# Pre-LN attention block with gated MLP: the end of each chunk through TensorE transposes, new ranks for residual sums and LN2, and the first K maximum from PSUM

## The chip, the cores and the metric

The kernel runs on one core of one Trainium2 chip. The metric is the device time of one execution in microseconds. Three runs of the kernel before gave 883.87, 884.46 and 886.01 us, median 884.46.

## The reference

One sequence of 2048 tokens, model width 640, 32 heads of 20, MLP width 1728, all inputs bf16. Random inputs are scaled by 0.05 (and the MLP weights by one over the root of their input width).

```python
def _A_ref(x, wqkv, wo):                       # attention
    qkv = (x @ wqkv).reshape(B, S, 3, H, Dh).transpose(2, 0, 3, 1, 4)
    q, k, v = qkv[0], qkv[1], qkv[2]
    scores = jnp.einsum("bhqd,bhkd->bhqk", q, k) * (Dh ** -0.5)
    p = softmax(scores)
    o = jnp.einsum("bhqk,bhkd->bhqd", p, v)
    return o.transpose(0, 2, 1, 3).reshape(B, S, D) @ wo

def _B_ref(x, w_gate, w_up, w_down):           # gated MLP
    return (gelu(x @ w_gate) * (x @ w_up)) @ w_down     # tanh form of gelu

h  = x + _A_ref(layernorm(x), wqkv, wo)
h2 = h + _B_ref(layernorm(h), w_gate, w_up, w_down)
```

The scores are 32 x 2048 x 2048 numbers, and each needs an exponential.

## The kernel before

**A planner writes the order.** The kernel first lists its operations (`op`) with engine, planned duration, priority, what each reads and writes, and which PSUM banks it takes and gives back. `Sched.schedule` then plays them through in planned time: whenever an engine is free it takes the ready operation with the lowest priority number (ties by the order of listing). `emit` writes each engine's program in exactly that order, with semaphore waits. So each engine's order is fixed before the kernel runs, and priorities act only through it. SP issues all DMAs, and one that has to wait holds back those behind it. `QK_LEAD`, `PE_AGE`, `SD_AGE`, `SD_ROW`, `DRAIN` are constants of this planner: how long before ScalarE runs dry TensorE takes no low-ranked work, how long an operation of another tiling mode may wait, and so on.

**Prologue.** x is loaded in four parts, normalized (LN1), transposed by TensorE into `xnT`. K and Q of the first group of four heads are projected first (`proj_k(0)`, `proj_q(0, 0)`). Scores are not shifted by their own row maximum: `q_bound0` computes a bound from the largest absolute value of each K row and |q|, and writes it into a spare row of Q, so the score matmul subtracts it. In `proj_k` this maximum takes, for each of four chunks of 512 columns, a copy from PSUM by ScalarE (L708), a bit mask on VectorE for the absolute value, a maximum with the first chunk's, and then one more fold and a reduction into `kd`; `sel0` is scaled by it and `q_bound0` multiplies.

**Middle.** The queries go in eight chunks of 512, 256 (five), 128 and 128 tokens. A chunk is worked in slots: chunk 0 has eight, a chunk of 256 four, one of 128 two; 32 slots (0 to 31) in all, each of 64 tiles of 128 keys x 512 scores. Slots 0 to 7 are chunk 0, slots 28 and 29 chunk 6, slots 30 and 31 chunk 7. `unit` takes tiles from the list by turns into three banks and two banks of PSUM (scores at L976, 32-row tiling) and lets ScalarE take the exponential of the whole unit into `pts` or `pts2`, a ring of `PR` + `PR2` tiles. `D_SLOT` gives the number of groups of four tiles in each slot whose exponential VectorE makes instead (`d_exp`): a conversion to int16 from PSUM (L889), then four shifted patterns whose bf16 readings sum to the exponential, each a separate operand of probability times V (`pv_op`); `SUMS` has some pairs of patterns added on VectorE first. All slots accumulate into one bank, bank 6; row 20 of each head holds the sum of the probabilities.

**End of a slot** (`epilogue`, `spread`): VectorE copies the bank to `osb`. For chunks 0 to 6 the sums go to DRAM and back in another layout, POOL takes reciprocals (ten instructions), these go to DRAM and come back broadcast over partitions (`bsum`), VectorE multiplies (`on16`, rank `P_ON`), and four DMAs write the rows to DRAM (`attn`). Chunk 7 (`tail`) does it with four fp32 TensorE transposes (L1063), a reciprocal (L1069) and products (L1072) into `o_nat`.

**After a chunk** (`post`): one DMA fetches the transposed attention output into `oT`, then follow the out projection, residual sum (L1124), LN2 statistics, a reciprocal root on POOL, `xn_t`, a DMA transpose into `hnT`, gate matmuls, gelu, up matmuls, product, down matmuls, the last sum into `ob` (L1228) and the output DMA. For chunks of 256 and more these matmuls run as four column tiles of 32 (`col4`, L676), for the last two chunks plain (L1158, L1223, L681). The work has ranks `P_LN` = 2.5 and `P_BG` = 3 and banks 5 and 7, so it fills the gaps that scores (0) and probability times V (1) leave; VectorE's patterns rank `P_EPI` = 2. `prefetch(c)` loads x of chunk c into its place of `h_sb`, which has room for four tiles of 128 tokens; chunks of 256 take its halves by turns. The MLP width is 13.5 tiles of 128: tile 13 overlaps tile 12 by half, and the doubled rows of w_down are zero.

Where TensorE would have nothing to do the planner writes matmuls whose results nobody uses (`warm`, operands from `kt_all`, and `pad`, zero weights added into bank 6).

The lines that the steps touch: `proj_qk` L701, `proj_k` L715, `q_bound0` L790, `proj_v` L802, `spread` L1023, `epilogue` L1044, `prefetch` L1078, `post` L1101.

## Time and profile before

| | us |
|---|---|
| median of three runs | 884.46 |
| profiled execution | 884.74 |
| its span | 883.0 |
| PE busy | 830.0 (94%) |
| ACT busy | 832.0 (94%) |
| DVE busy | 753.4 (85%) |
| POOL busy | 134.2 (15%) |
| mean share of the DMA engines in use | 20% |

PE is TensorE, ACT ScalarE, DVE VectorE, POOL GpSimd, SP SyncE, which issues the DMAs. A row of a group gives the line, the engine, the operation, what it writes from what, shapes and count; then busy time and the mean duration of one in ns; then the engine's idle time ahead of them and what ended it. The line can be that of a helper (L395 stands for all operations that were recorded through `I`). A row in order of time gives start, duration, engine, line, operation, and in brackets the idle time ahead of it. A row of stages gives, after the stretch and its length, the busy time and the number of instructions of PE, PE's weight loads, DVE, ACT and POOL, the clock granted to TensorE (1.00 is full speed), the DMA share and GB/s. Matmul durations of the profile include their pipeline, so matmuls that follow each other overlap.

### The profile page before, as it was taken

How to read it: one execution, taken by the hardware profiler on the slowest of the kernel's cores; microseconds unless marked ns; L12 is line 12 of the kernel's file. 1: busy time of each engine (PE TensorE's matmuls, PEld its weight loads, DVE VectorE, ACT ScalarE, POOL GpSimd, SP SyncE). 2: the span in 40 equal slices, each digit the busy share in tenths (PEclk: the TensorE clock that was granted, in tenths of full speed). 3: DMA queues.
4: the chain of work that ended last, by engine and by line, in shares of the span. 5: the costliest groups of instructions: out<-in, count | busy, mean ns of one | idle time of the engine just before them, and what ended most of it. 6: DMA issues, size and time to landing. Idle time of an engine off the chain costs nothing.

```text
span 883.0 us, 36651 instructions
## 1 busy us (share of the span) xinstructions
PE 830.0 (94%) x16658; PEld 405.4 (46%) x16658; DVE 753.4 (85%) x1356; ACT 832.0 (94%) x798; POOL 134.2 (15%) x431
## 2 busy tenths in 40 slices
PE   3999999999989899999999999999999999999998
PEld 1532222222234333344545555545554556666687
DVE  8839999999879889788899878999899997976864
ACT  6799999999999999999999999999999999999931
POOL 5001111110201201111031211113101321120200
PEclk9999999999999999999999999999999999999999
DMA  7211130332264410001121101101020101103000
GB/s 268 75 44 58 31 79 19 107 90 68 76 175 126 106 30 19 19 8 42 42 64 35 33 17 50 34 8 35 27 57 20 30 19 42 45 16 65 6 17 24
DMA packets 57298, 46.95 MB, mean 53 GB/s; under 512 B 25524, under 2 KB 50704, under 8 KB 57144
## 3 DMA queue, kind: packets, MB, share of 16 engines
q1 hardware_dynamic: 57144, 44.62, 19.2%
q8 instruction: 130, 2.13, 1.0%
q14 instruction: 24, 0.20, 0.1%
HBM read 30.68 MB, written 11.04 MB: 47 GB/s over the span
## 4 chain that ended last, share of the span: by engine, by line
ACT 56%; PE 28%; DVE 12%; POOL 1%; issue 1%; DMA 1%
ACT pts L395 44%; ACT rege L395 12%; PE ps L676 9%; PE ps L976 7%; PE ps L395 5%; PE ps L681 4%; DVE qt_all L395 3%; DVE rege L889 2%; PE ps L1158 2%; DVE rege L395 2%; DVE qt_all L889 1%; DVE stats L395 1%; PE ps L1223 1%; DMA rege<-xn_t 1%; ACT qt_all L395 1%
## 5 line engine op out<-in xcount | busy, mean ns | idle before, releaser
L395 ACT ACTIVATE pts<-ps 128x1024 bf16<-128x1024 f32 (+1 forms) x585 | 639.3, 1244 | 8.0 <-PE ps L976 6.1
L976 PE MATMUL ps<-qt_all,kt_all 32*128 32x256 bf16 (+2 forms) x4096 | 301.2, 272 | 24.3 <-ACT pts L395 17.5
L976 PEld LDWEIGHTS ps<-qt_all,kt_all 32*128 32x128 bf16 x4096 | 101.8, 92 | 227.1 <-ACT pts L395 150.5
L395 ACT ACTIVATE rege<-ps 128x1536 bf16<-128x1536 f32 (+1 forms) x129 | 178.6, 1401 | 1.7 <-PE ps L395 1.5
L889 DVE TENSOR_SCALAR rege<-ps 128x512 int16<-128x512 f32 x220 | 148.7, 682 | 27.9 <-PE ps L976 27.2
L676 PE MATMUL ps<-rege,regw 128*32 128x256 bf16 (+1 forms) x3360 | 152.4, 292 | 5.7 <-ACT rege L395 1.8
L395 PE MATMUL ps<-pts,v_all 128*21 128x256 bf16 (+2 forms) x2711 | 132.1, 273 | 0.3 <-ACT pts L395 0.2
L395 PE MATMUL ps<-rege,v_all 128*21 128x256 bf16 (+2 forms) x1877 | 130.1, 287 | 2.3 <-issue 1.5
L889 DVE TENSOR_SCALAR qt_all<-ps 128x512 int16<-128x512 f32 x136 | 92.2, 683 | 19.7 <-PE ps L976 18.8
L676 PEld LDWEIGHTS ps<-rege,regw 128*32 128x32 bf16 x3360 | 77.9, 96 | 44.5 <-issue 24.9
L395 DVE TENSOR_SCALAR rege<-rege 128x2048 int16<-128x2048 int16 x139 | 93.3, 684 | 2.5 <-PE ps L395 1.9
L681 PE MATMUL ps<-regw 128*128 128x512 bf16 (+1 forms) x360 | 90.2, 356 | 2.5 <-ACT regw L628 2.0
L395 POOL TENSOR_SCALAR rn<-rc 128x16 int32<-128x16 int32 x30 | 8.6, 288 | 526.2 <-DMA rc<-sums 525.8
L395 PEld LDWEIGHTS ps<-pts,v_all 128*21 128x21 bf16 x2711 | 62.4, 91 | 30.1 <-issue 23.3
L676 PE MATMUL ps<-regw,rege 128*32 128x320 bf16 x1568 | 74.7, 301 | 0.6 <-DVE rege L889 0.5
L395 DVE TENSOR_SCALAR qt_all<-qt_all 128x2048 int16<-128x2048 int16 (+2 forms) x118 | 68.8, 594 | 0.6
L395 PEld LDWEIGHTS ps<-rege,v_all 128*21 128x21 bf16 x1877 | 50.1, 91 | 36.4 <-issue 20.9
L395 PE MATMUL ps<-qt_all,v_all 128*21 128x256 bf16 (+1 forms) x1360 | 58.8, 262 | 0.5 <-DVE qt_all L395 0.3
L395 DVE TENSOR_SCALAR qt_all<-rege 128x2048 int16<-128x2048 int16 x83 | 56.2, 689 | 1.6 <-PE ps L395 1.0
L681 PEld LDWEIGHTS ps<-regw 128*128 128x128 bf16 x360 | 29.3, 99 | 51.1 <-issue 26.6
L1211 DVE TENSOR_TENSOR rege<-rege,ps 128x512 bf16<-128x512 bf16 (+1 forms) x53 | 35.8, 677 | 12.1 <-PE ps L676 11.2
L676 PEld LDWEIGHTS ps<-regw,rege 128*32 128x32 bf16 x1568 | 36.6, 96 | 19.0 <-issue 9.3
(113 smaller groups left out, 724.2 us busy)
## 6 DMA issues: line engine op xcount, KB each, us to landing
bsum<-rsums SPq DMA_DIRECT2D x120, 64.0 KB, 2.1
rege<-in_A_x_dram SPq DMA_DIRECT2D x5, 640.0 KB, 5.6
q_rows<-regw SPq DMA_DIRECT2D x20, 128.0 KB, 1.8
out_dram<-rege SPq DMA_DIRECT2D x16, 160.0 KB, 2.6
attn<-on SPq DMA_DIRECT2D x120, 20.0 KB
regw<-in_B_w_gate_dram SPq DMA_DIRECT2D x5, 432.0 KB, 3.6
regw<-in_B_w_up_dram SPq DMA_DIRECT2D x5, 432.0 KB, 3.3
kt_all<-k_rows SPq DMA_DIRECT2D x12, 160.0 KB
```

Source lines behind the costliest of these rows:

```text
L395: return lambda eng: getattr(eng, method)(*args, **kwargs)
L676: return [lambda eng, j=j: eng.matmul(out()[32 * j:32 * j + 32], l[:, 32 * j:32 * j + 32], r, start=start, stop=stop, tile_position=(0, 32 ...
L681: fn = col4(lambda: bank(bk, n), l, r, k == 0, k == len(steps) - 1) if col else lambda eng, l=l, r=r, k=k: eng.matmul(bank(bk, n), l, r, s ...
L889: d_ops.append(op("dve", lambda eng: eng.tensor_scalar(v[:, 512 * h:512 * h + 512], bank(b), EXP_MUL, -32000.0, ALU.mult, ALU.max), c_dve( ...
L976: return lambda eng: eng.matmul(out()[:, kk * nq:(kk + 1) * nq], kt_all[32 * j:32 * j + 32, g, kt * 128:(kt + 1) * 128], qt_all[32 * j:32 ...
L1158: lambda eng, a=a, f=f, fi=fi: eng.matmul(bank(bk)[:, fi * nq:(fi + 1) * nq], w[:, a, F0[f]:F0[f] + 128], hnT[:, a, 128 * tb:128 * tb + nq ...
L1211: hdone.append(op("dve", lambda eng, bu=bu, fv=fv, w=w: eng.tensor_tensor(fv, fv, bank(bu, w), ALU.mult), c_dve(w), p, reads=[ku] + hkeys( ...
L1223: f == NF - 1) if nq >= COL else lambda eng, f=f, o=o, hf=hf, bk=bk: eng.matmul(
```

## The change

- **Last slot of a chunk.** For chunks 1 to 6 the last slot, for chunk 0 slots 6 and 7, no longer go through DRAM. They take chunk 7's way (four fp32 transposes, reciprocal, products), into `wda` or `sq`, and small matmuls against the identity then transpose them into `oT`, with a VectorE copy. The other slots' rows still come by DMA, now two a chunk.
- **Ranks.** Out projection `P_OUT` 1.1, residual sums `P_ADD` 0.6, statistics and LN2 `P_ST` 0.7, the new transposes `P_NOW` 0.9 and their VectorE work `P_DV` 0.5, against 2.5 before. LN2 of chunks 0 and 3 is transposed by TensorE and copied by VectorE.
- **First K maximum.** VectorE reduces each chunk with absolute values to one column of `km`, the last one straight from PSUM before ScalarE copies it; one small reduction combines the four.
- **V.** Four first-half V tiles are copied by ScalarE (two before); VectorE's V copies and those of the second K tile wait for `sel0`. The second half of V moves from slots 0 to 2 to slots 1 and 2.
- **Last MLP tile.** For chunks of 256 and more tile 13 computes only its 64 columns, for both halves of the tokens at once, in half as many columns; `wda` holds the matching rows of w_down.
- **Output.** The last sum goes into `h_sb`, and the output DMA reads it there; `ob` is gone, and its space goes to `pts2`.
- **Numbers.** The ring has 13 + 6 tiles (12 + 4 before). Slot 30 has no VectorE tiles (two groups before). `SUMS`, `D_RING`, `D_SPAN` and the planner's constants get values by slot.

```diff
-PR, PR2 = 12, 4
-D_SLOT = (0,) + (3,) * 27 + (2, 3, 2, 1)
-SUMS = (0,) + (1,) * 6 + (0, 1, 1, 0) + (1,) * 5 + (2,) + (1,) * 10 + (0, 1, 1, 1, 0)
+PR, PR2 = 13, 6
+D_SLOT = (0,) + (3,) * 27 + (2, 3, 0, 1,)
+SUMS = (0,) + (1,) * 7 + (0, 1, 0,) + (1,) * 3 + (0, 1,) + (2,) * 3 + (1,) * 6 + (2, 1, 0, 1, 0, 1, 0,)
-VN = 6
-D_RING = (6,) * 26 + (4, 6, 12, 12, 0, 6)
-D_FIRST, D_SPAN = 0, 18
+VN = 3
+D_RING = (6,) * 8 + (9, 6, 6, 9,) + (6,) * 6 + (0, 6,) + (3,) * 7 + (6,) * 4 + (9,)
...
-V_ACT = (0, 1)
-XN_DVE = (9, 13, 15)
+V_ACT = (0, 1, 2, 3)
+XN_DVE = (12, 14, 15)
+HOLD = 1
+V_HOLD = 3
+XP_PE = (0, 3)
+P_NOW = 0.9
+P_K0 = 1.0
+P_DV = 0.5
+P_ADD = 0.6
+P_ST = 0.7
+P_OUT = 1.1
...
@@ proj_qk
-            if evac == "act":
+            if dkey[0] == "ku" and t == 0:
+                red = lambda src, r: op("dve", lambda eng: eng.tensor_reduce(km[:, c:c + 1], src(), AX.X, ALU.max, apply_absolute_value=True),
+                                        0.62, P_K0, reads=[r], writes=[("km", c)])
+                m = [red(lambda: bank(bk), key)] if c == 3 else []
+                e = op("act", lambda eng: eng.activation(dst, bank(bk), ACT.Copy), c_act(512), prio, reads=[key],
+                       writes=[dkey], rel=[bk], after=m)
+                if c < 3:
+                    w_readers.append(red(lambda: dst, dkey))
+            elif evac == "act":
...
@@ proj_k
+                op("dve", I("tensor_reduce", kd[:, 0:1], km[:], AX.X, ALU.max), 0.1, P_K0, reads=[("km", c) for c in range(4)],
+                   writes=[("kd", 0)])
...
@@ epilogue
-            if c < len(CHUNKS) - 1:
+            tail = c == len(CHUNKS) - 1
+            g_dir = [g for ss, (cc, gg) in enumerate(slots) if cc == c and (tail or gg[-1] == NG - 1 or c == 0 and gg[0] == NG - 2)
+                     for g in gg]
+            if gs[0] not in g_dir:
                 spread(s, c, gs, nq)
                 return
...
+            if tail or not last:
+                return
...
+            op("sp", I("dma_start", oT[:, 0:na, tok], src[0:128 * na, :].rearrange("(a p) s -> p a s", p=128)), 0.4, P_EPI,
+               reads=ars, writes=hk, sem=f"oT{c}", lat=O_LAT + nq * 0.004, after=tuple(e_ops) if c == 0 else ())
...
+                        fs = [lambda eng, i=i, a=a, tt=tt, q=q, b3=b3: eng.matmul(
+                            bank(b3)[q:q + 32, i * nq + tt * 128:i * nq + tt * 128 + 128],
+                            buf[:, tt, 128 * a + q - f0:128 * a + q - f0 + 32], ident[:], start=True, stop=True,
+                            tile_position=(0, q), skip_group_check=True) for q in range(p0, 128, 32)]
...
+                    op("dve", lambda eng, i=i, a=a, p0=p0, b3=b3: eng.tensor_copy(
+                        oT[p0:128, a, tok], bank(b3)[p0:128, i * nq:i * nq + nq]), c_dve(nq), P_DV, reads=[k3], writes=hk,
+                       rel=[b3] if i == len(part) - 1 else [])
@@ post
-                       c_dve(320), p, reads=[key, ("h", tt, hf)], writes=[("h", tt, hf)], rel=[bk], after=first)
-                ln_stats(h_sb[:, tt, :], t, [("h", tt, 0), ("h", tt, 1)], p)
+                       c_dve(320), p if tail else P_ADD, reads=[key, ("h", tt, hf)], writes=[("h", tt, hf)], rel=[bk], after=first)
+                ln_stats(h_sb[:, tt, :], t, [("h", tt, 0), ("h", tt, 1)], p if tail else P_ST)
...
-                if tail:
+                if tail or c in XP_PE:
                     transposes(xn_t[:, t % 2, :], [("xn", t % 2)], hnT[:, :, tt * 128:(tt + 1) * 128], ("hnT", tt),
-                               banks, p, "act", after=first)
+                               banks, p if tail else P_NOW, "act" if tail else "dve", after=first)
...
+                    half = nq >= COL and f == NF - 1
+                        fn = [lambda eng, a=a, fi=fi, j=j: eng.matmul(
+                            bank(bk)[32 * j:32 * j + 32, fi * nq:fi * nq + nq // 2], w[:, a, FL + 32 * (j % 2):FL + 32 * (j % 2) + 32],
+                            hnT[:, a, 128 * tb + j // 2 * (nq // 2):128 * tb + (j // 2 + 1) * (nq // 2)], start=a == 0, stop=a == NA - 1,
+                            tile_position=(0, 32 * j), skip_group_check=True) for j in range(4)] if half else col4(lambda fi=fi: bank(bk)[:, fi * nq:(fi + 1) * nq], w[:, a, F0[f]:F0[f] + 128],
...
-                        ob[:, i, hf * 320:(hf + 1) * 320], bank(bk, 320), h_sb[:, tt, hf * 320:(hf + 1) * 320], ALU.add),
-                       c_dve(320), p, reads=[key, ("h", tt, hf)], writes=[("ob", i, hf)], rel=[bk], after=first)
-                op("sp", I("dma_start", out_hbm[t * 128:(t + 1) * 128, :], ob[:, i, :]), 0.08, p,
+                        h_sb[:, tt, hf * 320:(hf + 1) * 320], bank(bk, 320), h_sb[:, tt, hf * 320:(hf + 1) * 320], ALU.add),
+                       c_dve(320), p, reads=[key, ("h", tt, hf)], writes=[("h", tt, hf)], rel=[bk])
+                op("sp", I("dma_start", out_hbm[t * 128:(t + 1) * 128, :], h_sb[:, tt, :]), 0.08, p,
```

More of the change, by code (lines that the diff above doesn't have):

```diff
@@ L260, in schedule @@
         self.order = order
-        self.span = max(o.fin for o in ops)
+        self.span = max(o.fin for o in self.order)
     def emit(self, es, block_of):
@@ L337 @@
 F0 = tuple(min(128 * f, DFF - 128) for f in range(NF))
+FL = 128 * (NF - 1)
 SCALE = DH ** -0.5
@@ L800, in q_bound0, with proj_v @@
             q_keys[0][0] = [("qo", 0, 0)]
-        def proj_v(kt, hf, banks, prio, evac="dve"):
+        def proj_v(kt, hf, banks, prio, evac="dve", after=()):
             bk = Bank(*banks)
```

197 lines of the change are left out of this document (125 added, 72 removed).

## The prediction, before the changed kernel was seen

> **What bounds the kernel now.** I read the busy time by stage first, then ScalarE's groups by shape, then the start and the end in order of time.
>
> ```profile
> core 0: us, PE busy (x) PEld busy (x) DVE busy (x) ACT busy (x) POOL busy (x), PEclk, DMA share, GB/s
> 0.00:37.00 37.00, 22.08 (x154) 12.34 (x154) 30.51 (x96) 24.60 (x45) 12.17 (x32) 1.00 0.52 176
> 37.00:842.10 805.10, 770.52 (x15813) 361.63 (x15816) 700.11 (x1209) 798.84 (x741) 122.05 (x399) 1.00 0.20 49
> 842.10:883.00 40.90, 37.43 (x700) 31.42 (x692) 22.73 (x52) 8.52 (x13) 0.00 (x0) 1.00 0.05 18
> ```
>
> Three stages, three limits. A prologue of 37.0 us ends with the first exponential. A middle of 805.1 us ends with the last one; there ACT is busy for 798.8 us, so it can be shortened by the 6.3 us of idle at most, or by giving ACT less. A tail of 40.9 us has ACT busy for 8.5 us and PE for 37.4: PE, and the chain of the last chunk, set it.
>
> ```profile
> L395 ACT ACTIVATE pts<-ps 128x1024 bf16<-128x1024 f32 x406 | 426.6, 1119 | 2.6 <-PE ps L976 1.4 <-PE ps L395 1.0
> L395 ACT ACTIVATE pts<-ps 128x1536 bf16<-128x1536 f32 x178 | 273.1, 1535 | 5.5 <-PE ps L976 4.8 <-PE ps L395 0.6
> L395 ACT ACTIVATE rege<-ps 128x1536 bf16<-128x1536 f32 x87 | 133.7, 1537 | 1.6 <-PE ps L395 1.5
> L395 ACT ACTIVATE rege<-ps 128x1024 bf16<-128x1024 f32 x42 | 44.9, 1120 | 0.0
> ```
>
> These are the exponentials. A further score tile of 512 columns costs 1535 - 1119 = 416 ns if it rides in an instruction that runs anyway.
>
> **The prologue.** From the last K chunk to the first exponential:
>
> ```profile
> 31.55 0.60 ACT L708 ACTIVATE regw<-ps 128x512 bf16<-128x512 f32 x1 [0.48 <-PE ps L681]
> 32.18 0.29 DVE L395 TENSOR_SCALAR rege<-regw 128x512 int16<-128x512 int16 x1 [0.22 <-ACT regw L708]
> 32.39 0.48 DVE L814 CAST v_all<-ps 128x320 bf16<-128x320 f32 x1
> ...
> 34.23 0.41 DVE L395 TENSOR_REDUCE kd<-rege 128x1 f32<-128x256 bf16 x1
> ...
> 35.54 0.75 DVE L797 SCALAR_TENSOR_TENSOR qt_all<-ps,off,qt_all 128x512 bf16<-128x512 f32 x1
> 37.02 4.63 ACT L395 ACTIVATE pts<-ps 128x1536 bf16<-128x1536 f32 x4 [3.58 <-PE ps L976]
> ```
>
> PSUM holds the chunk by 31.55. ACT copies it, VectorE takes the absolute value, folds twice and reduces, with three V copies like that at 32.39 in between, and is through at 34.64. The change reduces from PSUM at 31.55 and combines four values; VectorE's V copies, twelve now, wait for it. A 512-column reduction isn't shown. The 256-column one takes 0.41, so 0.41 to 0.82; I take 0.65 (twice the columns, one fixed part), and 0.2 for the combination. That ends near 32.45 in place of 34.64: 2.2 us earlier, 1.2 if an instruction already running or ACT's two added V copies come first, 2.8 if the K copies behind it go too. The wait that is added stands on ACT: its copy of this chunk now follows the reduction, and behind it the table load (1.28 us before) must be done before the exponential; 32.2 + 0.6 + 1.3 = 34.1 against 34.8 leaves room. **Minus 2.2.**
>
> The Trainium skill (VectorE: DVE Perf Modes, Rules for kernel authors) speaks against it: a reduction on a hot path only runs at the single rate and should be restructured. By that rule the old bit mask and folds would be the faster way, and the sum would be a few tenths worse. The trace bears it out only in rate: with 0.29 for the mask alone, fixed parts weigh more at these widths.
>
> **The middle.** Slot 30 gives up its two groups of VectorE tiles. Dealing out the tiles as the code does gives 714 exponentials on both sides, 448 of two tiles and 265 of three before, 442 and 272 after: eight tiles more on ACT, 8 x 0.416 = 3.3 us. Work of chunk 6 that now lies in the tail would move here:
>
> ```profile
> 860.96 1.79 ACT L395 ACTIVATE qt_all<-qt_all 128x1024 f16<-128x1024 f16 x2 [3.14 <-DVE qt_all L395]
> ```
>
> Two Tanh, 1.8 us, free in the tail and not in a full middle. The halved last feature tile takes 128 columns (256 in chunk 0) from the gelu of six chunks: 128 x 0.416/512 = 0.1 each, 0.7 in all. Nineteen probability tiles in place of sixteen can only shrink ACT's idle time; work ranked above probability-times-V can enlarge it. I leave it at 6.3; bounds -3 and +11 (a rival). **Plus 4.4.**
>
> **What the hops hold up.** At the end of chunks 0 and 6:
>
> ```profile
> 234.28 0.69 DVE L395 COPY osb<-ps 128x512 f32<-128x512 f32 x1 [0.45 <-PE ps L395]
> 266.75 0.59 PE L676 MATMUL ps<-wo,rege 128*32 128x320 bf16 x12
> 302.36 0.45 DVE L395 TENSOR_SCALAR xn_t<-rege,mu,rs 128x640 bf16<-128x640 bf16 x1
> 312.86 0.40 PE L676 MATMUL ps<-rege,regw 128*32 128x512 bf16 x4 [1.29 <-DMA rege<-xn_t]
> ...
> 786.68 0.69 DVE L395 COPY osb<-ps 128x512 f32<-128x512 f32 x1 [0.46 <-PE ps L395]
> 807.32 0.69 DVE L395 TENSOR_TENSOR on<-osb,bsum 128x512 bf16<-128x512 f32 x1
> 821.89 0.48 DVE L1124 TENSOR_TENSOR rege<-ps,rege 128x320 bf16<-128x320 f32 x1
> 836.98 0.44 DVE L395 TENSOR_SCALAR xn_t<-rege,mu,rs 128x640 bf16<-128x640 bf16 x1
> 845.83 1.39 PE L1158 MATMUL ps<-rege,regw 128*128 128x128 bf16 x22
> ```
>
> Chunk 0's attention ends at 234, its first gate matmul comes at 313; chunk 6 takes from 787 to 846. Without the hops four transposes, a reciprocal, the products, small transposes and copies stand between the copy and the out projection, about 5 us, and the residual sums no longer wait behind exponent patterns. Chunk 0 could start its gate near 263, 50 us earlier. What PE does meanwhile:
>
> ```profile
> 240.00:313.00 73.00, 63.08 (x1221) 26.64 (x1219) 62.77 (x109) 72.61 (x68) 12.45 (x43) 1.00 0.52 134
> 540.00:640.00 100.00, 95.94 (x2246) 49.54 (x2242) 94.28 (x163) 99.97 (x95) 19.93 (x61) 1.00 0.13 31
> ...
> L395 PE MATMUL ps<-kt_all 128*128 128x512 bf16 x31 | 10.0, 385 | 0.0
> L395 PE MATMUL ps<-kt_all,zer 128*32 128x512 bf16 x40 | 3.9, 380 | 0.0
> ```
>
> Between 240 and 313 PE has 9.9 us idle and 13.9 of matmuls whose result nobody reads. That is room for the MLP, but each bank of it (five steps of 512 columns; by 8.0 us for 56 steps of 320 below, 1.14 us) needs a VectorE copy of 0.69, and VectorE has 10.2 idle there, 15 copies: between PE's idle time alone and 15 banks, 10 to 17 us of MLP can come forward. I take 12, near the idle time, since the transposed work of later slots wants VectorE as well. The later chunks queue behind chunk 0, so the lead reaches the end if nothing eats it.
>
> **The tail.** What runs in it, and its own chain:
>
> ```profile
> L1158 PE MATMUL ps<-rege,regw 128*128 128x128 bf16 x280 | 16.6, 219 | 0.0
> L676 PE MATMUL ps<-regw,rege 128*32 128x320 bf16 x224 | 8.0, 299 | 0.0
> L1223 PE MATMUL ps<-regw,rege 128*128 128x320 bf16 x56 | 7.9, 299 | 0.5 <-DVE rege L1183 0.5
> L676 PE MATMUL ps<-rege,regw 128*32 128x256 bf16 x100 | 3.3, 273 | 0.1
> ...
> 842.85 0.68 DVE L395 COPY osb<-ps 128x512 f32<-128x512 f32 x1
> 845.34 0.66 PE L1063 MATMUL ps<-identf,osb 128*128 128x128 f32 x4
> 852.66 0.45 DVE L395 TENSOR_SCALAR xn_t<-rege,mu,rs 128x640 bf16<-128x640 bf16 x1
> 856.63 0.45 PE L622 MATMUL ps<-ident,xn_t 128*128 128x128 bf16 x5
> 857.12 0.70 ACT L628 ACTIVATE rege<-ps 128x640 bf16<-128x640 bf16 x1 [3.35 <-PE ps L622]
> 880.19 0.49 DVE L1228 TENSOR_TENSOR rege<-ps,rege 128x320 bf16<-128x320 f32 x1 [1.34 <-PE ps L1223]
> ```
>
> Chunk 7 needs half of 16.6 and half of 7.9. The rest is backlog: 8.3 + 4.0 of chunk 6, 8.0 + 3.3 of chunk 5, 23.6 us. It also delays the chain: transposes 845.34 - 843.53 = 1.8 late, 856.63 - 853.11 = 3.5 late. The floor without backlog: chain to 857.82 less those delays, 857.82 - 842.1 - 5.3 = 10.4; own gate, up and down 8.3 + 4.0; 0.5 wait, 0.5 last sum, 2.3 to the end: 26.0, or 14.9 less than now.
>
> Backlog taken away: 12 of lead; halving ten of each chunk's matmul steps, 256/320 x 8.0/56 / 2 = 0.057 each, 0.57 for each of chunks 1 to 5 and 1.14 for chunk 0, 4.0; slot 30's fewer probability-times-V groups, five of them:
>
> ```profile
> L395 PE MATMUL ps<-pts,v_all 128*21 128x128 bf16 x716 | 17.8, 220 | 0.1
> ...
> out_dram<-rege SPq DMA_DIRECT2D x16, 160.0 KB, 2.6
> ```
>
> 16 x 17.8/716 = 0.4 each at most, 1 to 2, say 1.5. Added: seven chunk ends at 0.66 + 0.45 of transposes, and six tiles of LN2 in chunks 0 and 3 that go through PE at 0.45 instead of a DMA, 10.5 us, more than half of it where PE has nothing to do: 4. On VectorE a chunk end swaps one 0.69 product for a reciprocal and products over 320 columns and copies of 512, by the 0.48 and 0.69 above 1.5 to 2; slot 30 frees it of 16 instructions of that size, which covers it. Backlog 23.6 - 13.5 = 10.1. Before 857.8 PE ran 12.0 us of backlog (3.3, 2.2 of chunk 6's gate, 6.5 of down), which cost the chain 5.3; 6.7 fits into its holes, 3.4 stays, and I leave 1 of delay: 26.0 + 4.4 = 30.4. **Minus 10.5** (0 to -14.9).
>
> **Queues.** Eight slots lose their eleven DMAs on SP and ten POOL instructions each; seven chunks fetch in two DMAs instead of one. Outputs leave from the residual buffer, so the next fetch into it waits for a 2.6 us landing; SP's hops of the running slot stand behind that, with twenty us to spare (786.68 to 807.32).
>
> **Sum.** The profiled execution took 884.74, 1.74 around its span: 884.74 - 2.2 + 4.4 - 10.5 = 876.4. The median shown, 884.46, is 0.3 below that execution: 876.
>
> **Rivals.**
> 1. *All of the lead arrives*: tail at 26.0, ACT idle down 2, prologue as above: 884.5 - 2.2 + 2.4 - 14.9 = 870. For it: halving and slot 30 help just where the backlog sits. Against: filler has delayed the chain by 5.3.
> 2. *VectorE eats the lead.* It is 94% busy from 540 to 640 and must empty every MLP bank; a lead needs VectorE, not PE. The residual buffer ties chunk c to the output of c - 2 besides. Then only chunk 6's shorter path, halving and slot 30 help the tail, 5: 884.5 - 2.2 + 4.4 - 5 = 882. The Trainium skill (TensorEngine Tiling (Array Packing), PSUM Bottleneck) has this rule: tiling speeds TensorE but not the emptying of PSUM. The 94% row agrees, the 240 to 313 row with 86% less so.
> 3. *Slower: the new ranks starve ACT.* Sums, statistics and transposes ahead of exponent patterns make the last VectorE terms of a slot late; the single accumulator bank stays taken, probability tiles pile up, and ACT waits. Nineteen tiles are eight instructions, about 8 us of cover; chunk 0's sums and statistics (8 x 0.48 and more) come near it. From 2 us lost at each of seven ends it decides: 876 + 14 = 890. Against: idle is only 6.3 now, and each such step is short.
> 4. *The transposes change nothing*, because backlog is taken first come first served: 885 with the eight tiles paid and a little tail won.
>
> **Chances.** Forecast (871 to 879) 0.45, rival 1 0.22, rival 2 0.14, rival 3 0.13, rival 4 0.06. One measurement can't tell 0.3%, 2.7 us, from no change. Rival 2 lies across that bound; faster 0.76, within 0.08, slower 0.16. Range 867 to 886: from below rival 1's 870 (prologue at -2.8, idle at -3) to just past rival 4; most of rival 3 is left out. The forecast's own range is 871 to 881.
>
> **What would show it.** Prologue: first exponential near 34.8. Middle: 442 and 272 exponentials, ACT busy about 803 of 807. Lead: chunk 0's first gate matmul before 270, unread matmuls between 240 and 313 mostly gone. Tail: about 30 us with under 12 us of other chunks in it. The prediction is wrong if ACT's idle time passes 12 us, or if chunks 5 and 6 still fill the tail.

## The result, and the profile after

Six runs of the changed kernel gave a median of 875.60 us (874.49 to 878.32), six of the kernel before beside them 884.29. The ratio is 0.9902 with a 95% interval of 0.9887 to 0.9917: 8.7 us faster. The profiled execution took 874.49 us, its span is 872.8. That execution is the fastest of the six. The view of busy time by stage, cut at the first and behind the last exponential, columns as before:

```profile
core 0: us, PE busy (x) PEld busy (x) DVE busy (x) ACT busy (x) POOL busy (x), PEclk, DMA share, GB/s
0.00:34.30 34.30, 19.57 (x146) 11.32 (x146) 28.41 (x88) 25.67 (x47) 11.61 (x30) 1.00 0.56 188
34.30:845.90 811.60, 787.25 (x16235) 378.42 (x16235) 707.07 (x1253) 805.80 (x742) 93.34 (x321) 1.00 0.17 44
845.90:872.80 26.90, 22.90 (x334) 19.27 (x330) 11.92 (x30) 7.48 (x12) 0.00 (x0) 1.00 0.04 14
```

The prologue went from 37.0 to 34.3 us (-2.7), the middle from 805.1 to 811.6 (+6.5), the tail from 40.9 to 26.9 (-14.0). Span: -10.2. The middle is still ScalarE's: 5.8 us of idle there, 6.3 before. Its exponentials, grouped by shape:

```profile
L427 ACT ACTIVATE pts<-ps 128x1024 bf16<-128x1024 f32 x296 | 306.3, 1068 | 1.9 <-PE ps L427 1.4 <-PE ps L1018 0.2
L427 ACT ACTIVATE pts<-ps 128x1536 bf16<-128x1536 f32 x199 | 296.8, 1491 | 2.3 <-PE ps L1018 1.9
L427 ACT ACTIVATE rege<-ps 128x1024 bf16<-128x1024 f32 x146 | 149.8, 1069 | 0.9 <-PE ps L1018 0.7
L427 ACT ACTIVATE rege<-ps 128x1536 bf16<-128x1536 f32 x73 | 108.5, 1487 | 0.7 <-PE ps L1018 0.6
```

442 of two tiles and 272 of three, as dealt out. The busy times of these groups sum to 861.4 us, more than ScalarE is busy in all, and 16.9 less than before (878.3), while ScalarE is busy 7.0 longer. So the records of successive exponentials overlap, and the mean of a group isn't what one costs. From start to start one takes 904 ns with two tiles and 1330 with three (903, 904 and 1330 are the most frequent distances in both traces; the medians are the same to 3 ns). By these the exponentials account for 757.9 us before (one of 512 columns among them, at 0.5) and 761.3 after, +3.4; ScalarE's other work between the first and the last for 28.4 and 28.6. What is left, 18.7 before and 21.6 after, is exponentials starting later than the pace: +2.9. Delays of more than 0.5 us add up to 5.3 us before and 3.1 after, the many smaller ones to 13.2 and 18.4.

The start, in order of time:

```profile
30.42 0.69 DVE L743 TENSOR_REDUCE km<-regw 128x1 f32<-128x512 bf16 x1 [0.39 <-ACT regw L746]
31.02 0.68 DVE L743 TENSOR_REDUCE km<-ps 128x1 f32<-128x512 f32 x1
31.74 0.16 DVE L427 TENSOR_REDUCE kd<-km 128x1 f32<-128x4 f32 x1
31.74 0.60 ACT L746 ACTIVATE regw<-ps 128x512 bf16<-128x512 f32 x1 [1.35 <-DVE km L743]
31.93 0.51 DVE L427 TENSOR_SCALAR sel<-sel,kd 128x4 bf16<-128x4 bf16 x2
32.81 1.28 ACT L427 ACT_TABLE_LOAD   x1
34.31 2.37 ACT L427 ACTIVATE pts<-ps 128x1536 bf16<-128x1536 f32 x2 [0.22 <-PE ps L1018]
```

From the start of the last reduction to that of `sel0` it is now 31.93 - 31.02 = 0.91 us, and 3.29 to the first exponential. The kernel before took 37.02 - 31.55 = 5.47 from the copy of that K quarter. The ends of chunks 0 and 6:

```profile
232.32 0.69 DVE L427 COPY osb<-ps 128x512 f32<-128x512 f32 x1 [0.47 <-PE ps L427]
239.74 0.31 PE L711 MATMUL ps<-wo,rege 128*32 128x320 bf16 x4
258.62 0.48 DVE L1202 TENSOR_TENSOR rege<-ps,rege 128x320 bf16<-128x320 f32 x1
270.70 0.44 DVE L427 TENSOR_SCALAR xn_t<-rege,mu,rs 128x640 bf16<-128x640 bf16 x1
275.52 0.39 PE L711 MATMUL ps<-rege,regw 128*32 128x512 bf16 x4
...
785.86 0.68 DVE L427 COPY osb<-ps 128x512 f32<-128x512 f32 x1
801.19 0.72 PE L716 MATMUL ps<-wo,rege 128*128 128x320 bf16 x4
831.76 0.61 PE L1240 MATMUL ps<-rege,regw 128*128 128x128 bf16 x8 [0.34 <-DVE rege L1313]
```

Chunk 0's first gate matmul (L711, from `regw`) comes at 275.5 instead of 312.9, chunk 6's (L1240) at 831.8 instead of 845.8. The two stretches of the middle that the prediction read, by windows:

```profile
240.00:313.00 73.00, 71.00 (x1445) 31.70 (x1443) 67.52 (x121) 72.91 (x68) 11.98 (x44) 1.00 0.35 100
540.00:640.00 100.00, 97.72 (x2375) 54.01 (x2367) 98.82 (x183) 99.97 (x96) 15.61 (x44) 1.00 0.08 23
```

TensorE between 240 and 313, grouped by line:

```profile
L711 PE MATMUL ps<-rege,regw 128*32 128x512 bf16 x220 | 16.7, 382 | 0.0
...
L427 PE MATMUL ps<-kt_all,zer 128*32 128x512 bf16 x28 | 2.6, 384 | 0.0
L427 PE MATMUL ps<-kt_all 128*128 128x512 bf16 x7 | 2.2, 385 | 0.0
```

There 16.7 us of MLP now run (220 matmuls, 55 steps of four), unread matmuls shrank from 13.9 to 4.8 us, and TensorE's idle time from 9.9 to 2.0. Last, TensorE in the tail, grouped from 845.9 on:

```profile
L1240 PE MATMUL ps<-rege,regw 128*128 128x128 bf16 x206 | 12.3, 219 | 0.6 <-DVE rege L1313 0.6
L1308 PE MATMUL ps<-regw,rege 128*128 128x320 bf16 x56 | 8.1, 299 | 0.5 <-DVE rege L1266 0.5
```

Chunk 7 itself needs 140 of the first and 28 of the second group. So 66 matmuls (66/206 of 12.3, 3.9 us) and 28 down matmuls (half of 8.1, 4.1) of chunk 6 are left; nothing of chunk 5. The 66 are fewer than chunk 6's 70 up matmuls, so its gate matmuls are done. Backlog: 8.0 us, 23.6 before. Chunk 6's two Tanh, of its gelu, are through at the end of attention too (the last exponential ends at 845.9):

```profile
842.55 1.06 ACT L427 ACTIVATE qt_all<-qt_all 128x1024 f16<-128x1024 f16 x1
845.89 0.84 ACT L427 ACTIVATE qt_all<-qt_all 128x768 f16<-128x768 f16 x1
```

In the kernel before they start 18.9 and 19.9 us after the last exponential. The tail in order of time:

```profile
847.24 0.69 DVE L427 COPY osb<-ps 128x512 f32<-128x512 f32 x1
857.46 7.99 PE L1240 MATMUL ps<-rege,regw 128*128 128x128 bf16 x140 [0.59 <-DVE rege L1313]
865.97 3.98 PE L1308 MATMUL ps<-regw,rege 128*128 128x320 bf16 x28 [0.52 <-DVE rege L1266]
869.98 0.49 DVE L1313 TENSOR_TENSOR rege<-ps,rege 128x320 bf16<-128x320 f32 x1 [1.41 <-PE ps L1308]
```

Attention's end to the first gate matmul takes 11.6 us, gate and up 8.5, down and last sum 4.5, the output 2.3. Most of the backlog runs in the holes of the first 11.6 us.

### The profile page after: what moved, and what is told of

The parts are those of the page before. It is cut to its first block, busy times and chain, and to the rows that moved or that the text cites. A ratio compares the mean times of both kernels' runs of the same rounds, so it can differ in the third digit from the quotient of the medians.

```text
span 872.8 us, 36588 instructions
## 1 busy us (share of the span) xinstructions
PE 829.7 (95%) x16710; PEld 409.0 (47%) x16710; DVE 747.4 (86%) x1371; ACT 838.9 (96%) x800; POOL 105.0 (12%) x351
## 4 chain that ended last, share of the span: by engine, by line
ACT 57%; PE 36%; DVE 6%; issue 1%; DVEq 0%
ACT pts L427 38%; ACT rege L427 18%; PE ps L1018 10%; PE ps L427 8%; PE ps L711 8%; PE ps L716 5%; PE ps L1240 2%; DVE qt_all L427 1%; DVE rege L931 1%; ACT qt_all L427 1%; PE ps L1308 1%; DVE rege L427 1%; DVE stats L427 1%; PE ps L652 1%; ACT L427 0%
## 5 line engine op out<-in xcount | busy, mean ns | idle before, releaser
L427 ACT ACTIVATE pts<-ps 128x1024 bf16<-128x1024 f32 (+1 forms) x495 | 557.7, 1238 | 4.2 <-PE ps L1018 2.0
L1018 PE MATMUL ps<-qt_all,kt_all 32*128 32x256 bf16 (+2 forms) x4096 | 306.3, 272 | 13.0 <-ACT pts L427 7.8
L427 ACT ACTIVATE rege<-ps 128x1024 bf16<-128x1024 f32 (+1 forms) x219 | 248.4, 1208 | 1.6 <-PE ps L1018 1.3
L931 DVE TENSOR_SCALAR rege<-ps 128x512 int16<-128x512 f32 x216 | 146.5, 684 | 28.4 <-PE ps L1018 28.0
L711 PE MATMUL ps<-rege,regw 128*32 128x256 bf16 (+1 forms) x3120 | 140.7, 292 | 3.4 <-DVE rege L931 1.0
L427 PE MATMUL ps<-pts,v_all 128*21 128x256 bf16 (+2 forms) x2411 | 119.7, 272 | 0.1
L931 DVE TENSOR_SCALAR qt_all<-ps 128x512 int16<-128x512 f32 x132 | 89.1, 684 | 18.5 <-PE ps L1018 18.1
L711 PEld LDWEIGHTS ps<-rege,regw 128*32 128x32 bf16 x3120 | 73.4, 96 | 38.1 <-issue 17.6
L711 PE MATMUL ps<-regw,rege 128*32 128x320 bf16 x1512 | 76.3, 301 | 1.3 <-DVE rege L1294 0.6
L427 PEld LDWEIGHTS ps<-pts,v_all 128*21 128x21 bf16 x2411 | 53.8, 91 | 31.2 <-issue 25.2
L427 DVE TENSOR_SCALAR qt_all<-qt_all 128x2048 int16<-128x2048 int16 (+3 forms) x116 | 66.6, 590 | 1.6 <-ACT qt_all L427 0.9
L711 PEld LDWEIGHTS ps<-regw,rege 128*32 128x32 bf16 x1512 | 35.2, 96 | 20.8 <-issue 11.6
L1294 DVE TENSOR_TENSOR rege<-rege,ps 128x512 bf16<-128x512 bf16 (+2 forms) x53 | 34.8, 658 | 9.0 <-PE ps L711 8.4
```

Source lines behind the costliest of these rows:

```text
L427: return lambda eng: getattr(eng, method)(*args, **kwargs)
L711: return [lambda eng, j=j: eng.matmul(out()[32 * j:32 * j + 32], l[:, 32 * j:32 * j + 32], r, start=start, stop=stop, tile_position=(0, 32 ...
L931: d_ops.append(op("dve", lambda eng: eng.tensor_scalar(v[:, 512 * h:512 * h + 512], bank(b), EXP_MUL, -32000.0, ALU.mult, ALU.max), c_dve( ...
L1018: return lambda eng: eng.matmul(out()[:, kk * nq:(kk + 1) * nq], kt_all[32 * j:32 * j + 32, g, kt * 128:(kt + 1) * 128], qt_all[32 * j:32 ...
L1294: hdone.append(op("dve", lambda eng, bu=bu, fv=fv, w=w: eng.tensor_tensor(fv, fv, bank(bu, w), ALU.mult), c_dve(w), p, reads=[ku] + hkeys( ...
```

## The experiments

Each is the changed kernel with one or two parts undone. Stages are cut as above in each one's profiled execution. The column "net" is the time from the first exponential to the end of the span, compared with the changed kernel's 838.5: the start of one and the same order varies by more than a microsecond between executions (first exponential at 34.3 to 35.8 in ten kernels with the same start, of which the changed kernel's is the earliest), and net leaves that out. The median of the kernel before was 884.8 to 885.6 in these comparisons, so ratios are given.

| run | prologue | middle | tail | net | median | ratio to before, 95% |
|---|---|---|---|---|---|---|
| before | 37.0 | 805.0 | 40.9 | +7.5 | 884.3 | |
| after | 34.3 | 811.6 | 26.9 | 0 | 875.6 | 0.990 (0.989 to 0.992) |
| a_hops | 35.5 | 811.3 | 33.5 | +6.3 | 881.9 | 0.996 (0.995 to 0.998) |
| a_ranks | 35.2 | 811.7 | 30.8 | +4.0 | 879.4 | 0.993 (0.991 to 0.996) |
| a_hopsranks | 35.0 | 807.7 | 38.9 | +8.1 | 883.8 | 0.999 (0.997 to 1.000) |
| a_slot30 | 35.8 | 806.6 | 33.9 | +1.9 | 877.9 | 0.992 (0.990 to 0.995) |
| a_slot30_1 | 35.1 | 809.5 | 31.0 | +2.1 | 876.6 | 0.990 (0.988 to 0.992) |
| a_nohalf | 35.4 | 812.2 | 31.9 | +5.5 | 880.4 | 0.996 (0.994 to 0.998) |
| a_kold | 35.6 | 811.5 | 27.0 | 0 | 875.6 | 0.989 (0.987 to 0.992) |
| a_hold0 | 35.8 | 815.3 | 31.1 | +7.9 | 883.3 | 0.998 (0.996 to 0.999) |
| a_vhold | 35.1 | 811.5 | 26.9 | -0.1 | 875.9 | 0.988 (0.985 to 0.991) |
| a_ring | 35.4 | 825.8 | 29.2 | +16.5 | 890.9 | 1.007 (1.005 to 1.010) |
| a_ringranks | 34.4 | 822.4 | 29.2 | +13.0 | 887.9 | 1.002 (1.001 to 1.004) |
| a_tables | 34.9 | 821.0 | 28.2 | +10.6 | 885.5 | 1.000 (0.998 to 1.001) |

A warning for all of them: the planner makes a new order for the whole kernel from each edit, and the tables by slot fit the changed kernel's order. What an edit costs can include this.

Two of the profiled executions also hold 6.8 us in which TensorE's granted clock is 0.50. In a_hopsranks they lie in the tail:

```profile
854.20:861.00 6.80, 5.75 (x52) 5.47 (x53) 3.36 (x8) 2.92 (x5) 0.00 (x0) 0.50 0.00 0
```

All ten executions of a_hopsranks have a mean clock of 0.996 to 0.998, so its median has this in it as well. In a_ring they lie in the middle, at 786.7 to 793.5; two of its four executions have it (892.1 and 892.2 us), two have the full clock (888.5 and 889.7).

### The hops and the ranks

The DMA hops put back for the last slots (a_hops):

```diff
-            if gs[0] not in g_dir:
+            if not tail:
                 spread(s, c, gs, nq)
...
+            if not tail:
+                op("sp", I("dma_start", oT[:, :, 128 * tb:128 * tb + nq],
...
```

> The changed kernel with the DMA hops back for every slot of chunks 0 to 6 (all else as changed). Lead theory (the changed kernel gained its tail because the MLP of each chunk starts earlier): chunk 0's first gate matmul goes from about 275 us back past 295, chunk 6's residual sums from 803 past 812, backlog of chunks 5 and 6 in the tail rises from 7 to 12 us or more, the tail from 26.9 to 30 to 38, the middle gets 1 to 3 us shorter because TensorE is less crowded; 878 to 885 in all. Rival (VectorE sets the MLP's pace, and the tail gained by slot 30 and the halved tile alone): first gate later, but tail under 29 and 874 to 877 in all. Rival (no use at all): 875 to 876 with the middle unchanged.

The ranks put back (a_ranks), and both (a_hopsranks):

```diff
-P_ADD = 0.6
-P_ST = 0.7
-P_OUT = 1.1
+P_ADD = 2.5
+P_ST = 2.5
+P_OUT = 2.5
```

> The changed kernel with out projection, residual sums, statistics and LN2 back at rank 2.5 (transposes at chunk ends kept). Lead theory: the distance from the end of a chunk's attention to its LN2 grows by 10 us or more, tail 29 to 34, 877 to 882. Rival (the new ranks starve ScalarE and cost the middle its unexplained 2.8 us): the middle falls from 811.6 to 809 or less, and the total to 874 or less if the tail holds. Rival (ranks do nothing): within 1 us of 875.6.

> Both back: hops, and rank 2.5. Lead theory: nearly the old flow of the MLP with slot 30, halved tile and prologue still new: tail 33 to 39, middle 808 to 810, 880 to 885. Rival (VectorE sets the pace): tail under 30, total under 877. If the middle's unexplained 2.8 us come from the crowd of earlier MLP work on TensorE, they are gone here: ScalarE's middle at 808.8 or less.

The tail grew by 6.6, 3.9 and 12.0 us, the middle in none of them (with both undone it is 3.9 shorter; with the hops alone 1 to 3 less were expected and 0.3 came). Chunk 0's first gate matmul came at 298.6, 280.6 and 305.7 (275.5 in the changed kernel), chunk 6's out projection at 821, 802 and 816 (801). The start of LN2's last step (`xn_t`) by chunk, in us:

| run | 0 | 1 | 2 | 3 | 4 | 5 | 6 |
|---|---|---|---|---|---|---|---|
| before | 302 | 453 | 501 | 601 | 692 | 792 | 837 |
| after | 267 | 411 | 468 | 570 | 668 | 763 | 813 |
| a_hops | 291 | 429 | 490 | 593 | 689 | 788 | 832 |
| a_ranks | 272 | 413 | 481 | 577 | 681 | 763 | 814 |
| a_hopsranks | 299 | 442 | 490 | 593 | 703 | 787 | 828 |

So every chunk's end is earlier, and without the hops it is so by about 20 us at each. The ranks do little at chunks 0 and 1 (5 and 2 us, where 10 or more were expected) and 8 to 14 at chunks 2 to 4: that part of the lead isn't one that chunk 0 begins. Whether chunk 0's lead alone would reach the end was not tried.

What makes the tail longer can be read there. TensorE's groups in the tail with both undone:

```profile
L1245 PE MATMUL ps<-rege,regw 128*128 128x128 bf16 x280 | 18.9, 234 | 0.0
...
L711 PE MATMUL ps<-regw,rege 128*32 128x320 bf16 x20 | 1.0, 299 | 0.0
```

All 140 gate and up matmuls of chunk 6 and some down matmuls of chunk 5 are in it. That is not all of the backlog of before, which had 224 down and 100 gate or up matmuls of chunk 5; and the 280 took 18.9 us instead of 16.6 before, 2.3 more, in the stretch at half clock. The same reading for all runs with a longer tail (Tanh: starts after the last exponential's end; the last column is TensorE idle or with unread matmuls):

| run | tail | gate and up matmuls of chunks 6 and 7 | chunk 6's Tanh | no useful matmul |
|---|---|---|---|---|
| after | 26.9 | 206, 12.3 us | -3.3 and 0.0 | 4.0 |
| a_hops | 33.5 | 251, 15.0 us | 7.2 and 8.2 | 8.0 |
| a_ranks | 30.8 | 221, 13.2 us | 3.0 and 5.9 | 7.2 |
| a_hopsranks | 38.9 | 280, 18.9 us | 9.1 and 13.1 | 9.8 |
| a_slot30 | 33.9 | 260, 16.0 us | 6.6 and 11.4 | 7.4 |
| a_slot30_1 | 31.0 | 230, 13.5 us | 3.6 and 5.9 | 6.7 |
| a_nohalf | 31.9 | 239, 14.2 us | 4.7 and 6.2 | 7.1 |

More matmuls left are one part of each longer tail. The other part, the larger one in four of these six runs, is about 3 to 6 us more in which TensorE stands or does unread work. In all six chunk 6's gelu has slipped into the tail; a_hops has a wait of 1.65 us for a VectorE product there. That this slip makes the empty time is read from the order, not tried by itself.

So the earlier ends of the chunks do shorten the tail. With both undone the median is 0.999 of before (interval up to 1.000), but that holds the half clock too: without 2.3 us of it, an estimate from the 280 matmuls alone, net would be +5.8, no more than with the hops alone. That the rest of the change gains nothing without the earlier ends is therefore not shown.

### Slot 30

VectorE's two groups put back (a_slot30), and one of the two (a_slot30_1, a 1 in that place):

```diff
-D_SLOT = (0,) + (3,) * 27 + (2, 3, 0, 1,)
+D_SLOT = (0,) + (3,) * 27 + (2, 3, 2, 1,)
```

> The changed kernel with slot 30's two groups of VectorE tiles back (eight tiles less on ScalarE). Lead theory: the tail is at its floor with 7 us of backlog hidden in the chain's holes, VectorE is busy for 33 of the last 57 us, so the 3.3 us of exponentials come back almost whole: middle about 808.5, tail 27 to 29, 872.5 to 875.5. Rival (the relief at the end is what made the tail): tail above 31, total above 877.

> The changed kernel with one exponent-pattern step of VectorE in slot 30 instead of none (before: two). Two steps gave middle 806.6 and tail 33.9, none gives 811.5 and 26.9. Theory A, each tile moved between ScalarE and VectorE is worth its own time and the two ends trade evenly: middle 809, tail 29.5 to 30.5, median 876 to 877.5. Theory B, the tail falls only while VectorE's patterns hold up chunk 5's and 6's MLP, and one step leaves that room: middle 809, tail 27 to 28, median 873 to 875, better than both kernels. Theory C, the tables by slot fit slot 30 without such steps only: middle 811 or more, tail over 30, median over 878.

Two groups: middle -5.0, tail +7.0; one: -2.0 and +4.1. The first theory (tail 27 to 29) failed; the rival's numbers came. TensorE's groups in the tail with two:

```profile
L1240 PE MATMUL ps<-rege,regw 128*128 128x128 bf16 x260 | 16.0, 219 | 1.3 <-DVE sd L427 0.8 <-ACT rege L658 0.5
...
L711 PE MATMUL ps<-regw,rege 128*32 128x320 bf16 x28 | 1.3, 299 | 0.0
```

54 gate or up matmuls more than in the changed kernel, and chunk 5 is back. Two things are in this. At 806.6 us after the first exponential, when attention ends in a_slot30, the changed kernel still has 233 of these matmuls to start and none of chunk 5, against 260 and 20: it is ahead at the same moment. In the 5 us by which its middle is longer it starts another 31. So about half of the backlog that is gone went into the room of a longer middle, and about half was done already by then. VectorE's patterns and their terms of probability times V are gone from slot 30; which of the two engines this relieved was not tried. The two terms are one as far as time goes: the net is 2 us. The hoped-for optimum at one group isn't there: net +2.1 with one, +1.9 with two.

### The halved steps

```diff
-                    half = nq >= COL and f == NF - 1
+                    half = False
```

> The changed kernel with full-width last steps of the MLP matmuls again (chunks 0 to 6), nothing else. The prediction priced the halving at 4.0 us of backlog, 0.57 for each of chunks 1 to 5 and 1.14 for chunk 0. Theory A, every microsecond of MLP matmul taken from a chunk arrives at the end: first exponential as in the changed kernel (34 to 36), middle unchanged within 1 us, tail 30 to 32 instead of 26.9, median 879 to 881. Theory B, TensorE has room in the middle and the lead of the chunks now absorbs it: tail 27 to 28, median within 1 of 875.6, so that the halving was not needed once the chunk ends were shortened.

Tail +5.0, middle +0.6: the numbers of the first theory, by a little more than priced (4.0). But the mechanism isn't that every microsecond of matmul arrives at the end. TensorE's group in this run's tail:

```profile
L1240 PE MATMUL ps<-rege,regw 128*128 128x128 bf16 x239 | 14.2, 219 | 0.0
```

33 matmuls more than in the changed kernel are left, 1.9 us, and no other MLP group is longer; the rest of the added work the middle took. The other 3.1 us of the tail are TensorE without useful matmuls (7.1 against 4.0), with chunk 6's Tanh 4.7 and 6.2 us after the last exponential.

### The start

The old K maximum (a_kold) in the new start:

```diff
-            if dkey[0] == "ku" and t == 0:
+            if False:
...
+                    s16 = ka[:, 512 * c:512 * c + 512]
...
+                op("dve", I("tensor_reduce", kd[:, 0:1], ka[:, 0:256], AX.X, ALU.max), 0.33, P_K0, reads=[("ka0", 0), "ka"],
```

> The changed kernel with the first K maximum done the old way (sign bits masked off, three maxima of 512 columns, a fold to 256, then the reduction), with all else of the new start (V copies held behind sel0, their order) as it is. Theory A, the chain of reductions is what the first exponential waits for: first exponential at 36 to 37.5 instead of 34.3, the rest unchanged, median 877 to 878.5. Theory B, the start is set by other work (the held copies and their order), the chain being hidden: first exponential at 34.3 to 35.2, median within 1 of 875.6.

Its start, in order of time:

```profile
30.98 0.60 ACT L751 ACTIVATE regw<-ps 128x512 bf16<-128x512 f32 x1 [0.48 <-PE ps L716]
32.72 0.42 DVE L427 TENSOR_REDUCE kd<-rege 128x1 f32<-128x256 bf16 x1
33.25 0.51 DVE L427 TENSOR_SCALAR sel<-sel,kd 128x4 bf16<-128x4 bf16 x2
35.60 2.37 ACT L427 ACTIVATE pts<-ps 128x1536 bf16<-128x1536 f32 x2 [0.47 <-PE ps L1026]
```

From the copy of the last quarter: 2.27 us to `sel0` and 4.62 to the first exponential. So of the 2.18 that the chain lost (5.47 to 3.29), the reduction from PSUM made 1.33, and the held V and K copies, with the rest of the new start, 0.85. The rest is unchanged to 0.1 us. But the medians don't show the 1.3: 875.59 and 875.60. It is about as large as the variation of the start (34.3 to 35.8; a_kold's 35.6 lies in it), and stays a result of the profile alone.

The hold taken away (a_hold0), and loosened by two V tiles (a_vhold):

```diff
-HOLD = 1
+HOLD = 0
```

```diff
-V_HOLD = 3
+V_HOLD = 5
```

> The changed kernel without the rule that holds V copies behind sel0. Theory A, the hold buys the early start and pays for it with the 1.42 us wait of ScalarE at 44.1 (probability times V late because its V copies are late): first exponential 0.7 to 2 us later, that wait below 0.4, sum within 1 us of the changed kernel. Theory B, the hold is not what makes the start early: first exponential within 0.5 of 34.3 and the wait gone, median 873.5 to 875. Theory C, the wait at 44 has another cause: it stays, and the start moves later, median 876.5 to 878.

> The changed kernel with V copies held from the sixth on instead of from the fourth (two more of them early). Theory A, the wait of 1.42 us at 44.1 comes from the held copies, and two more early ones remove half of it or all without moving the start by more than 0.7: wait below 0.8, median 874.5 to 876. Theory B, a shift of a microsecond at the start changes the planner's order everywhere behind it, as the run without the hold showed (4 us each in middle and tail): the wait shrinks and the median is 877 to 884 all the same. Theory C, the wait stays at 1.4: probability times V there waits for something other than these copies.

Both ask about the largest wait of ScalarE in the middle, in the changed kernel's order of time:

```profile
44.09 5.54 ACT L427 ACTIVATE pts<-ps 128x1024 bf16<-128x1024 f32 x5 [1.42 <-PE ps L427]
```

None of the three theories had a_hold0's 883.3. Without the hold the chain to the first exponential takes 3.74 instead of 3.29 us, and the wait is gone, but middle and tail are 3.7 and 4.2 longer: waits of 1.05, 1.29 and 1.28 us stand at 463, 466 and 521, far from the start. With two more early V tiles the wait stays at 1.42 and nothing else changes. So that the held V copies cause it, as I had thought, isn't borne out. What it waits for can be read in TensorE's order of time:

```profile
43.43 1.03 PE L427 MATMUL ps<-pts,v_all 128*21 128x512 bf16 x13
```

These are the first matmuls of probability times V, 9 us after the first exponential. Until they have run, the ring of 19 tiles has no room for the next unit. Without the hold the first eight come at 41.00, and with a smaller ring (a_ring, below) the same wait is 3.20 us. Why TensorE begins them so late is open; the hold also covers the K copies of the second tile, which were not freed by themselves. The 7.9 of the first run can't be the hold's own price at the start either. Its order is behind long before the waits at 463: chunk 0's first gate matmul comes at 291.5 instead of 275.5. What sets it back there is open.

### The ring and the tables

The ring back at 12 and 4 tiles (a_ring), and with the ranks back as well (a_ringranks):

```diff
-PR, PR2 = 13, 6
+PR, PR2 = 12, 4
```

> The changed kernel with the probability ring back at 12 and 4 tiles instead of 13 and 6; nothing else. The prediction gave the ring no price. Theory A, a probability tile is not what ScalarE waits for: middle within 1 us of the changed kernel's 777.2 (34.3 to 811.5), median 875 to 877. Theory B, the ring covers the bunched work at the ends of the chunks, where the new ranks put sums and statistics ahead of VectorE's exponent patterns: middle 2 to 5 us longer, median 878 to 881.

> The ring of 12 and 4 tiles with the three ranks (residual sums, statistics, output) back at 2.5: the two parts undone together that alone gave 890.9 (ring, middle 825.8) and 879.4 (ranks, middle 811.7). Theory A, the larger ring is the cover for the new ranks (rival 3, held off by the ring): without them the smaller ring is enough, middle 810 to 814, median 879 to 884. Theory B, the ring covers something else, the held V copies and the tables by slot made for it: middle 823 to 828, the waits at 44 and 171 us stay, median 891 to 896.

(The 777.2 of the first expectation takes the middle's length, 811.5, for its end.) With the small ring the middle is 14.3 us longer, part of it perhaps the half clock at 786.7 to 793.5, and the kernel is slower than before also in the two executions at full clock. The largest wait, in order of time:

```profile
162.82 5.26 ACT L427 ACTIVATE pts<-ps 128x1024 bf16<-128x1024 f32 x5
168.62 0.62 PE L427 MATMUL ps<-kt_all,zer 128*32 128x512 bf16 x8
169.36 1.29 DVE L427 TENSOR_SCALAR rege<-rege 128x2048 int16<-128x2048 int16 x2
170.69 0.61 PE L427 MATMUL ps<-rege,v_all 128*21 128x512 bf16 x7
171.35 1.45 ACT L427 ACTIVATE rege<-ps 128x1536 bf16<-128x1536 f32 x1 [3.28 <-PE ps L427]
```

At the end of a slot VectorE's last patterns are late; probability times V waits for them (TensorE adds zeros at 168.6), no probability tile comes free, and ScalarE stands 3.28 us. No chunk is finished at 171, so no sum or statistic stands in VectorE's way. The wait near 44 us is about as long, 3.20. With the ranks put back both are there too, 3.57 us at 170.6 and 3.20 at 43.7, and the middle is 822.4, 10.8 longer than the changed kernel's, at full clock throughout. So the ring is not the cover of the ranks, as the first theory had it, but of VectorE's pattern work and of the late start of probability times V as the changed kernel orders them; the median came 3 us lower than the second theory had it.

The tables by slot back at the values of before (a_tables; ring, transposes and ranks stay):

```diff
-PE_AGE = (2.5, 1.5,) + (3.5,) * 5 + (2.5, 2.5, 1.5, 2.5, 2.5,) + (1.0,) * 8 + (5.0,) + (1.0,) * 5 + (3.5, 3.5, 1.0, 1.0, 3.5, 1.0,)
+PE_AGE = 3.5
...
-D_RING = (6,) * 8 + (9, 6, 6, 9,) + (6,) * 6 + (0, 6,) + (3,) * 7 + (6,) * 4 + (9,)
+D_RING = (6,) * 26 + (4, 6, 12, 12, 0, 6)
...
```

> The changed kernel with every table by slot back at the values of before: the planner's lead, its three age limits, the engine of the probability sums, the ring shares and the spread of VectorE's patterns. Kept are the transposes without hops, the new ranks, slot 30's tiles, the halved steps, the start and the ring of 13 and 6. Theory A, the named parts of the change are what shortens the tail and the tables only trim the middle: tail 27 to 30, middle 812 to 818, median 877 to 883. Theory B, the tables carry the gain, and the named parts without them starve ScalarE as rival 3 has it: middle over 820, median 886 or more. Theory C, the tables do nothing: median within 1 of 875.6.

The tail stays short (28.2), and the middle is 9.4 longer: both theories have a part. Behind the start, waits of 0.7 us and more stand at 262, 264, 416, 419, 517, 573 and 673, all but the one at 517 between a chunk's out projection and its LN2. The longest:

```profile
562.90 0.48 DVE L1202 TENSOR_TENSOR rege<-ps,rege 128x320 bf16<-128x320 f32 x1
563.90 0.88 DVE L427 BATCH_NORM_STATS2 stats<-rege 128x6 f32<-128x320 bf16 x2
568.51 0.88 DVE L427 BATCH_NORM_STATS2 stats<-rege 128x6 f32<-128x320 bf16 x2
571.06 0.68 DVE L427 TENSOR_SCALAR qt_all<-rege 128x2048 int16<-128x2048 int16 x1
572.18 0.39 PE L427 MATMUL ps<-qt_all,v_all 128*21 128x256 bf16 x8
572.84 1.02 ACT L427 ACTIVATE pts<-ps 128x1024 bf16<-128x1024 f32 x1 [2.21 <-PE ps L427]
```

Sums and statistics of chunk 3 stand among the exponent patterns on VectorE from 562.9 to 570, the slot's last pattern runs at 571.06, probability times V at 572.18, and ScalarE has stood for 2.21 us. That is what rival 3 of the prediction describes. Statistics are about 1 of the 3.7 us between the last two patterns (566.7 and 571.1); conversions and MLP products take the rest. So the ranks are a part of it, and no run has the old tables together with the old ranks. The tables keep such waits away in the changed kernel, in which ScalarE has no wait over 0.3 us between 45 and 769. Which of the seven tables does it was not tried.

No version beat the changed kernel: a_vhold, a_kold and a_slot30_1 lie within the spread of its runs.

## Why the prediction was right

Time (876 against 875.6) and direction came out, the sum by terms that were each too small: -2.2, +4.4 and -10.5 against -2.7, +6.5 and -14.0. That the total fits so closely is in part luck: the middle was missed by 2.1 us one way, tail and prologue by 4.0 the other.

- **Prologue.** The step was right: the chain lost 2.18 us. A reduction of 512 columns took 0.68 (estimate 0.65), the combination 0.16 (0.2). The other 0.5 is an earlier last K quarter (31.02 against 31.55), which most other executions of this start didn't have (31.1 to 32.5). By the rule of the Trainium skill (VectorE: DVE Perf Modes, Rules for kernel authors) to restructure a reduction on a hot path, the mask and folds would have been the better way; a_kold has them, and they took 2.27 us where the reductions took 0.91.
- **Middle.** The counts were right, and the eight tiles cost 3.4 (3.3). Of the 1.1 for chunk 6's Tanh less the gelu saved 0.2 came. The step that failed is "I leave it at 6.3": idle time did stay, but exponentials start 2.9 us later in sum than their pace, by many delays of under 0.5 us. With hops and ranks put back the delays are those of before (18.6 us), with one of them they stay (22.2 and 22.6); which step makes them is open. Room in ScalarE's time isn't only in what the idle column shows.
- **Lead.** Chunk 0's gate was forecast near 263 and before 270, and came at 275.5. The out projection began 7.4 us after the copy (5 forecast), but the sums, statistics and LN2 took until 270.7: the eight sums, among VectorE's patterns, run from 242.3 to 258.6, and with the old ranks (a_ranks) they take the same 16.3 us. POOL's reciprocal root adds about 5 us from 260.8. The lead still filled the stretch: 55 steps of gate matmuls are 12.6 us by the prediction's own price (1.14 for five), where 12 were taken; their busy time of 16.7 includes their pipeline. "The later chunks queue behind chunk 0" isn't all of it: the ranks make most of their lead at chunks 2 to 4.
- **Tail.** The floor of 26.0 was right; 26.9 was measured. Mis-sized was what stands above it: 10.1 of backlog forecast and 4.4 us of it felt, 8.0 found and 0.9 felt. The term "slot 30, say 1.5" was the worst: undoing it costs the tail 7.0, about half because a longer middle is also room for MLP work. Halving was priced at 4.0 and costs 5.0 when undone, but only 1.9 of that as matmuls left over. The sum had no term for what it does to the tail whether chunk 6's gelu falls before or behind the end of attention. The parts undone one by one add up to 22.5 (6.6 + 3.9 + 7.0 + 5.0), more than the 14.0 gained, so they are not independent.
- **Rivals.** Rival 1 had the tail right, but not the middle. Rival 2 fell: VectorE is 99% busy from 540 to 640, and TensorE did more work there all the same (97.7, 95.9 before). Rival 4 fell with a_hops. Rival 3's kind of wait is real, and with the old tables the gain is gone (a_tables, 885.5); the prediction argued against it from short steps and the idle time, and named the ring as cover. What held it off were the tables, to which it gave no price; nor did it price the ring, without which the middle is about 11 to 14 us longer.

## What to carry to other kernels

Where background work of one engine fills the gaps of another's main loop, the length of the loop and the work left behind it trade against each other: price a shift between two engines by the time from the loop's start to the end of the kernel, not by each stage. Ask also at which step the last background work stands when the loop ends: a dependent step that slips behind it lengthens the tail by more than its matmuls. Work pulled forward in rank needs cover where it pushes something back; look for the operand that becomes late, the ring that is full behind it and the engine that stands, before counting the gain. In a kernel whose order is planned, test a part by undoing it and by keeping it with the old tuning: either alone tells half. And look at the granted clock of an execution before reading a difference of a few us from it.

## What the runs showed of the hardware

A reduction of 512 columns with absolute values takes VectorE the same time from PSUM in fp32 as from SBUF in bf16: 0.68 us at 31.02, 0.69 at 30.42. The records of ScalarE's exponentials hold time in which the next one already runs: with two tiles their mean fell from 1119 to 1068 ns while the pace from start to start stayed at 904. In the changed kernel's trace those that start within 5 ns of the pace have records of 1090 ns in the mean, those that start over 50 ns late 1040; that doesn't explain the whole fall, for on the pace it was 1137 before. And the granted clock can fall to 0.50 for 6.8 us in the midst of an execution at full clock: 280 matmuls around such a stretch took 18.9 us instead of 16.6.
